# Weight conversion spread differently over the first batch: first weight from chunk 1 on, its scratch in another buffer, more of the second beside the first products, unread products in the mixing's wait

## Chip, cores and metric

The kernel runs on one core of one Trainium2 chip. The time is the device time of an execution in microseconds (us). The engines are named as in the profile: PE (TensorE, matmul; PEld its weight loads), DVE (VectorE), ACT (ScalarE), POOL (GpSimd) and SP (SyncE, which only issues DMAs here).

## The reference, cut to what matters

```python
# attention: B=4, H=8, S=768, D=48, a recurrence over time
for t in range(S):
    y[:, :, t] = q_t @ state
    state += beta_t * outer(kn_t, v_t - kn_t @ state)      # kn = normalized key
x = y, heads side by side                                  # (4, 768, 384)
# mixing and channel network
u = x + real(fft2(x))                                      # over sequence and channels
un = (u - mean) / sqrt(var + 1e-6)
out = u + relu(un @ w_ch1) @ w_ch2                         # 384 -> 1536 -> 384
```

The two weights lie in memory as 64-bit floats (the inputs are numpy's float64), [...]. So the kernel converts them itself, from pairs of 32-bit words.

## The kernel before

**Attention in chunks.** Each batch of 768 rows is cut into 6 chunks of 128 rows (`NL` = 6), so there are 24 chunks. Four chunks form a round, and each round needs the inversion of many small triangular matrices, which DVE does step by step (`invert16` with lines L519 and L522 for rounds 0 to 2, `invert` with L448 and L452 for rounds 3 to 5). An inversion begins with the transpose L477 (or L407) and ends with the transposes L525 and L527 (or L455, L456). For each chunk, `pre_a` turns the keys and forms their Gram matrices, `pre_q` turns the queries and makes the masked product `LQ` (L557), `pre_m16` or `pre_m` makes the matrix `MT` (PE products `one<-Z,GU`, `one<-MT,ND`, `one<-Z,ND`; DVE lines L647 and L651), `step` carries the state through the two halves of the chunk (DVE lines L722 or L700, and L741), and `outputs` forms the rows of `x`.

**Mixing and network.** When a batch has its rows, `folds` makes sums and differences of rows and columns on DVE (L797 to L815), `fourier` multiplies by tables (PE `pf`/`one<-evt`, `odt`, then `one<-dtab,F`), adds the result to `x` and takes mean and variance (L884 to L892). `mlp` normalizes (L911, tile `un`), turns on PE (`ptr`) and ACT (L922, tile `unT`), and makes the first products `ph`, evicted by ACT as `hT` (L932), and the second products `po`. The network is done in three groups of 256 rows per batch; a group has 12 first products of three matmuls each. In the trace each fp32 matmul counts as two instructions.

**Order.** All is written in the order in which it shall run: generators stop at `yield`, and `advance`, `drain` and lists of them weave chunks, inversions and network together. PE's, DVE's, ACT's and POOL's order is the written one (`manual_schedule`). For chunks 6 and 7 only PE's order is written, and a scheduler sets that of the others. SP's order of DMAs is the scheduler's as well.

**The conversion** is the generator `weights()`: 12 pieces of 128x384 numbers for `w1`, then 12 for `w2`. A piece is loaded (64-bit, 384 KB) into a ring and takes two half-steps. On ACT: L278 (low word), later L283 and L284 (exponent). On DVE: L279 (upper mantissa), then L295, L299 and L301, and L291, the product that writes the result. L291 comes one half-step pair after L301 of its piece for `w1` (two scratch tiles), two pairs after for `w2` (three). Scratch for `w1` are two pool buffers: tag `M`, of which there is one and which each inversion needs, and tag `unT`, of which there are two. For `w2` ring and scratch lie in tiles `E` and `O3` of batch 0's folds. `convert(n)` takes half-steps of `w1`: none in chunk 0 and 1, 5 in chunk 2, 6 in chunk 3, 4 in chunk 4, then 7 around the mixing and the rest among the first products:

```python
rest = [ms[6], k1, ms[7], k1, ms[7], ms[6], k2, ms[7], k2, ms[7], k3, k3]
for fc in range(KF):
    if converted < 2 * KF + 2:
        convert(2)
    else:
        advance(conv)
    advance(side)
```

`conv` then goes on in `period(6)`, beside the third inversion.

**Unread products.** `spin(n)` issues n products of 128x384 that nothing reads, three at the start and six before the first `pre_m16`. They have one PSUM buffer of the two of tag `post` and read a tile of zeros, `idle`.

Of the kernel before, what the change touches and what calls it, by code (L numbers as in the profile page):

```python
# [10 lines left out]
F32 = mybir.dt.float32  # L11
I32 = mybir.dt.int32
U32 = mybir.dt.uint32
AX = mybir.AxisListType
ALU = mybir.AluOpType
ACT = mybir.ActivationFunctionType
# [48 lines left out]
def kernel(  # L65
# [10 lines left out]
    nc = tc.nc  # L76
    B, H, S, D = q.shape
    DM = H * D
    DFF = moe_w_ch1.shape[1]
    NL = S // L  # L80
# [3 lines left out]
    KF = DFF // 128  # L84
# [11 lines left out]
    wk = ctx.enter_context(tc.tile_pool(name="wk", bufs=1))  # L96
# [9 lines left out]
    def ps_post(shape, name):  # L106
        return ps.tile(shape, F32, tag="post", bufs=2, name=name)
# [83 lines left out]
    w2 = const.tile([128, KF, DM], F32, name="w2")  # L191

    early = w2.rearrange("p c m -> p (c m)").rearrange("p (n h d) -> p n h d", h=8, d=64)
    idle = wk.tile([128, DM], F32, tag="un", bufs=2, name="idle")
# [15 lines left out]
    evt = const.tile([128, TH, 2 * NE], F32, name="evt")  # L210
    odt = const.tile([128, TH, 2 * NO], F32, name="odt")
    dtab = const.tile([ND + 1, 4, ND + 1], F32, name="dtab")
    w1 = const.tile([128, KD, DFF], F32, name="w1")
# [7 lines left out]
    half_n = const.tile([128, GT], F32, name="half_n")  # L221
    nc.gpsimd.memset(half_n, -0.5)

    def weights():

        if moe_w_ch1.dtype == F32:
            nc.sync.dma_start(out=w1, in_=moe_w_ch1.rearrange("(c p) f -> p c f", p=128))
            nc.sync.dma_start(out=w2, in_=moe_w_ch2.rearrange("(c p) m -> p c m", p=128))  # L230
            return
        w1v = moe_w_ch1.bitcast(I32).rearrange("(c p) (f two) -> p c f two", p=128, two=2)
        w2v = moe_w_ch2.bitcast(I32).rearrange("(c p) (m two) -> p c m two", p=128, two=2)
        n = DM
        sets = [
            [(w1v[:, :, i:i + 128], w1[:, :, i:i + 128]) for i in range(0, DFF, 128)],
            [(w2v[:, i:i + 1], w2[:, i:i + 1]) for i in range(KF)]]
        for last, pieces in enumerate(sets):
            if last:

                E, O3 = spare.pop()
                ring = E.rearrange("p e t m -> p (e t m)").bitcast(I32).rearrange(
                    "p (i m two) -> p i m two", m=n, two=2)
                tmp = O3.rearrange("p e t m -> p (e t m)").rearrange("p (i e m) -> p i e m", e=2,
                                                                    m=n)
                tmp = [tmp[:, i] for i in range(3)]
                deep = 3
            else:
                ring = wk.tile([128, 4, n, 2], I32, tag="big", bufs=2, name="w64")
                tmp = None  # L250
                deep = 4

            def stage(i):
                if i < len(pieces):
                    src = pieces[i][0]
                    nc.sync.dma_start(
                        out=ring[:, i % deep].rearrange("p (c f) two -> p c f two",
                                                        c=src.shape[1]), in_=src)

            for i in range(deep):  # L260
                stage(i)
            yield
            if tmp is None:
                tmp = [wk.tile([128, 2, n], F32, tag="M", name="wtmp0"),
                       wk.tile([128, 2, n], F32, tag="unT", bufs=2, name="wtmp1")]

            def of(i):
                t = tmp[i % len(tmp)]
                return ring[:, i % deep, :, 0], ring[:, i % deep, :, 1], t[:, 0], t[:, 1].bitcast(I32)


            lag = len(tmp) - 1
            for i in range(len(pieces) + lag):
                if i < len(pieces):
                    lo, hi, man, num = of(i)


                    nc.scalar.activation(man, lo.bitcast(U32), ACT.Copy, scale=2.0 ** -52, bias=1.0)  # L278
                    nc.vector.tensor_scalar(num, hi, 0xFFFFF, None, op0=ALU.bitwise_and)  # L279
                if 0 < i <= len(pieces):  # L280

                    num0 = of(i - 1)[3]
                    nc.scalar.activation(num0, num0, ACT.Relu, scale=-1.0, bias=edges[:, 0:1])  # L283
                    nc.scalar.activation(num0, num0, ACT.Relu, scale=-2.0 ** 23,  # L284
                                         bias=edges[:, 1:2])
                yield
                if i >= lag:
                    _, _, man0, num0 = of(i - lag)
                    dst = pieces[i - lag][1]
                    c = dst.shape[1]  # L290
                    nc.vector.tensor_tensor(dst, man0.rearrange("p (c f) -> p c f", c=c),  # L291
                                            num0.bitcast(F32).rearrange("p (c f) -> p c f", c=c),
                                            op=ALU.mult)
                if i < len(pieces):
                    nc.vector.scalar_tensor_tensor(man, num, 2.0 ** -20, man, op0=ALU.mult,  # L295
                                                   op1=ALU.add)

                    man = man.bitcast(I32)
                    nc.vector.scalar_tensor_tensor(man, hi, -2 ** 31, man, op0=ALU.bitwise_and,  # L299
                                                   op1=ALU.bitwise_or)  # L300
                    nc.vector.tensor_scalar(num, hi, 20, 0x7FF, op0=ALU.logical_shift_right,  # L301
                                            op1=ALU.bitwise_and)
                    stage(i + deep)
                yield

# [510 lines left out]
    folded, spare = {}, []  # L818
# [141 lines left out]
    def advance(gen, n=1):  # L960
        for _ in range(n):
            if next(gen, "end") == "end":
                return False
        return True

    def drain(gen):
        for _ in gen:
            pass
# [20 lines left out]
    def part(gen, n):  # L989

        for _ in range(n):
            if next(gen, "end") == "end":
                return
            yield
# [7 lines left out]
    def period(g, side):  # L1002
# [48 lines left out]
        for i in range(SLOTS):  # L1051
# [9 lines left out]
            if li == 1 and i == 1 and r > 1 and not last_round:  # L1061
                inv = invert(r + 1)
            if g == NL:
                advance(inv, 4)
                advance(conv, 3 if i < 4 else 4)
            elif inv:
                advance(inv, 8 if r + 1 < R16 else 6)
            if n + 2 >= NL and 0 < i < 5:
# [21 lines left out]
    with tc.manual_schedule(engines=engines):  # L1090
# [3 lines left out]
        inv0, inv1 = invert16(0), invert16(1)  # L1094
        qs = [pre_q(g, QT6[:, g], LQ6[:, g]) for g in range(NL)]
        ms = [pre_m16(g) for g in range(2 * RL)]
        unread = ps_post([128, 512], "unread")

        def spin(n):

            for _ in range(n):
                nc.tensor.matmul(unread[:, 0:DM], lhsT=idle[:, 0:128], rhs=idle, start=True,  # L1102
                                 stop=True, skip_group_check=True)

        spin(3)
# [13 lines left out]
        load_v(1, nc.gpsimd)  # L1119
        load_q(4)  # L1120
        load_q(5)
        conv = weights()
        advance(conv)

        for g in range(RL, 2 * RL - 1):
# [7 lines left out]
        drain(inv0)  # L1133
        advance(keys[-1])
        spin(6)

        advance(ms[0])
        drain(keys[-1])
# [10 lines left out]
        advance(ms[1])  # L1149
        drain(ms[0])  # L1150
        advance(inv1, 5)
        first = part(conv, 2 * KF + 2)
        converted = 0
        fold = fd = iter(())

        def convert(n):
            nonlocal converted
            advance(first, n)
            converted += n

        def fill(n):

# [6 lines left out]
        for g in range(NL - 1):  # L1169
# [22 lines left out]
            else:  # L1192
                advance(c0)
                fill(4)
                if g == 2:
                    drain(inv1)
                    advance(n2)
                if g > 1:
                    convert(1)
                advance(nm)  # L1200
                advance(late)
                advance(c0)
# [7 lines left out]
                advance(nm)  # L1210
                advance(c1)
                fill(3)
                if g > 1:
                    convert(2)
                drain(nm)
                advance(n2)
                advance(c1)
                fill(3)
                if g == 4:
                    advance(n2)  # L1220
                    drain(qs[g + 1])
                    convert(1)
                elif g > 1:
                    convert(1)
                    advance(n2)
                    convert(2 if g == 3 else 1)
                else:
                    advance(n2)
                if g != 4:
                    drain(qs[g + 1])  # L1230
                if g + 2 < NL:
                    advance(qs[g + 2])
# [13 lines left out]
        g = NL - 1  # L1246
# [16 lines left out]
        load_beta(2)  # L1263

        advance(ms[6])
        f = fourier(0)
        advance(f)
        drain(fold)
        convert(1)
        advance(f, 4)  # L1270
        convert(1)
        advance(f, 2)
        side, done = mlp(0), 0
        advance(side)
        advance(ms[6])
        advance(ms[7])
        advance(side)
        convert(3)
        advance(ms[7])
        convert(2)  # L1280

        k1, k2, k3 = keys[1:]
        rest = [ms[6], k1, ms[7], k1, ms[7], ms[6], k2, ms[7], k2, ms[7], k3, k3]
        for fc in range(KF):
            if converted < 2 * KF + 2:
                convert(2)
            else:
                advance(conv)
            advance(side)
            if fc % 3 == 1:  # L1290
                advance(f)
            drain(rest[fc]) if fc == 5 else advance(rest[fc])
        drain(f)
        nq = pre_q(NL)
        advance(nq)
        for m in ms[6:] + keys[1:]:
            drain(m)
        advance(side)
# [54 lines left out]
```

## Time and profile before

| | us |
|---|---|
| median of 3 runs | 760.12 (756.09 to 760.19) |
| profiled execution | 761.02 |
| its span, first to last instruction | 758.9 |
| PE busy | 696.9 (92%) |
| DVE busy | 378.6 (50%) |
| ACT busy | 263.7 (35%) |
| POOL busy | 69.7 (9%) |

The shares are means over stages with different limits, so a stage is read from its own stretch of time. Batch 0's steps run from about 45 to 121 us, its mixing from 121 to 138, its first group of first products from 142 to 176; batches 1 to 3 follow. A line of a group gives busy time, mean ns of one instruction, and idle time before it; a line of the timeline gives start, duration and, in brackets, the idle time before and what ended it.

### The profile page before, as it was taken

To read this page: it belongs to the slowest core of one execution; us is meant where nothing else is said; L and a number is where in the kernel's file an instruction comes from. 1 tells how busy PE (TensorE), PEld (TensorE's weight loads), DVE (VectorE), ACT (ScalarE), POOL (GpSimd) and SP (SyncE) were. 2 spreads that over 40 slices of the span, in tenths; PEclk is the share of its full clock that TensorE was granted. 3 is DMA by queue.
4 is the path that set the end of the run, shared out by engine and by line. 5 is a ranking of instruction groups with operands and counts; after the bars stand their busy time and mean duration, and the time that the engine had idled before them with its cause. 6 is when DMAs were issued, how large, how long until landed. Compare 5 with 4: busy or idle time off the path is not lost.

```text
span 758.9 us, 23039 instructions
## 1 busy us (share of the span) xinstructions
PE 696.9 (92%) x10170; PEld 538.0 (71%) x10170; DVE 378.6 (50%) x957; ACT 263.7 (35%) x644; POOL 69.7 (9%) x114
## 2 busy tenths in 40 slices
PE   6877879598989987999999999999999999999998
PEld 4677868476767655877857767868667678777684
DVE  5867776669932499433198327278512240600000
ACT  5544663568623321223422323223223221211120
POOL 7000000100000011001110210020100110100000
PEclk8698797799999999999999999999999999999999
DMA  9842352014312322002222211001220000000000
GB/s 152 215 74 41 88 135 83 18 54 124 87 29 55 60 44 44 12 11 47 52 45 48 44 34 39 1 13 42 43 44 12 13 12 0 22 1 21 11 10 22
DMA packets 111862, 36.09 MB, mean 48 GB/s; under 512 B 101873, under 2 KB 109842, under 8 KB 111762
## 3 DMA queue, kind: packets, MB, share of 16 engines
q1 hardware_dynamic: 109938, 33.86, 20.5%
q8 instruction: 80, 1.31, 0.7%
q0 software_dynamic: 640, 0.43, 0.4%
q10 hardware_dynamic: 1184, 0.33, 0.3%
q14 instruction: 20, 0.16, 0.1%
HBM read 29.88 MB, written 4.72 MB: 46 GB/s over the span
## 4 chain that ended last, share of the span: by engine, by line
PE 75%; DVE 16%; ACT 5%; issue 2%; DMA 1%; POOL 0%; DVEq 0%; ACTq 0%; POOLq 0%
PE po L110 23%; PE ph L110 21%; PE one L110 16%; PE pair L110 10%; PE one L113 2%; DVE M L452 1%; DVE tmp L448 1%; DVE w L291 1%; PE ptr L113 1%; PE unread L1102 1%; PE pf L110 1%; DMA C<-in_k_dram 1%; DVE M L522 1%; DVE Z L647 1%; DVE tmp L519 1%
## 5 line engine op out<-in xcount | busy, mean ns | idle before, releaser
L110 PE MATMUL ph<-unT,w 128*128 128x256 f32 x864 | 207.7, 392 | 2.8 <-ACT hT L932 2.0
L110 PE MATMUL po<-w,hT 128*128 128x384 f32 x576 | 205.1, 495 | 0.0
L110 PEld LDWEIGHTS ph<-unT,w 128*128 128x128 f32 x864 | 162.4, 194 | 27.6 <-ACT hT L932 2.4
L110 PEld LDWEIGHTS po<-w,hT 128*128 128x128 f32 x576 | 103.7, 190 | 56.7 <-issue 0.3
L932 ACT ACTIVATE hT<-ph 128x256 f32<-128x256 f32 x144 | 54.9, 382 | 145.0 <-PE ph L110 144.9
L943 DVE TENSOR_TENSOR x<-x,po 128x384 f32<-128x384 f32 x24 | 13.2, 550 | 107.0 <-PE po L110 107.0
L741 DVE TENSOR_TENSOR S<-S,pair 128x192 f32<-128x192 f32 x40 | 14.0, 349 | 73.9 <-PE pair L110 73.9
L110 PEld LDWEIGHTS one<-V,MT 64*64 64x64 f32 x768 | 30.5, 141 | 19.5 <-issue 9.2
L884 DVE TENSOR_TENSOR x<-x,one 128x193 f32<-128x193 f32 x24 | 8.5, 354 | 69.8 <-ACT Q L875 69.8
L110 PE MATMUL one<-V,MT 64*64 64x48 f32 x768 | 35.7, 227 | 3.6 <-DVE V L700 1.8
L452 DVE TENSOR_TENSOR M<-M,tmp 128x31 f32<-128x31 f32 (+15 forms) x93 | 34.7, 373 | 3.2
L448 DVE TENSOR_TENSOR tmp<-A,M 128x31 f32<-128x31 f32 (+15 forms) x93 | 34.2, 367 | 2.5
L110 PE MATMUL one<-MT,ND 64*64 64x64 f32 x768 | 30.4, 231 | 5.0 <-DVE x L885 2.6
L110 PEld LDWEIGHTS one<-MT,ND 64*64 64x64 f32 x768 | 27.8, 146 | 6.0 <-ACT Q L875 3.0
L700 DVE TENSOR_TENSOR V<-V,pair 128x192 f32<-128x192 f32 x33 | 11.5, 350 | 38.7 <-PE pair L110 35.4
L110 PEld LDWEIGHTS one<-dtab,F 97*128 97x128 f32 (+1 forms) x192 | 25.2, 191 | 5.2 <-ACT F L879 0.5
L110 PEld LDWEIGHTS pair<-U,K 64*64 64x64 f32 x704 | 16.6, 139 | 17.4 <-issue 14.9
L322 ACT ACTIVATE QT<-one 128x512 f32<-128x512 f32 x24 | 14.3, 594 | 38.9 <-PE one L113 38.7
L110 PE MATMUL one<-dtab,F 97*128 97x97 f32 (+1 forms) x192 | 25.9, 275 | 0.0
L110 PE MATMUL pair<-KT 48*32 48x64 f32 (+1 forms) x1152 | 21.1, 238 | 5.1 <-ACT KT L322 3.8
L110 PEld LDWEIGHTS pair<-S,KT 48*64 48x64 f32 x528 | 10.7, 133 | 20.1 <-issue 10.8
L710 ACT ACTIVATE U<-one 128x192 f32<-128x192 f32 x36 | 11.9, 330 | 37.7 <-PE one L110 37.7
(176 smaller groups left out, 1003.0 us busy)
## 6 DMA issues: line engine op xcount, KB each, us to landing
w<-in_moe_w_ch_dram SPq DMA_DIRECT2D x12, 384.0 KB, 5.6
E<-in_moe_w_ch_dram SPq DMA_DIRECT2D x12, 384.0 KB, 4.3
out_dram<-x SPq DMA_DIRECT2D x24, 192.0 KB, 1.9
K<-in_k_dram SPq DMA_DIRECT2D x92, 48.0 KB, 2.7
V<-in_v_dram SPq DMA_DIRECT2D x92, 48.0 KB, 2.2
C<-in_k_dram SPq DMA_DIRECT2D x18, 192.0 KB, 9.3
Q<-in_q_dram SPq DMA_DIRECT2D x18, 192.0 KB, 3.1
w<-in_q_dram SPq DMA_DIRECT2D x6, 192.0 KB, 7.5
```

Source lines behind the costliest of these rows:

```text
L110: nc.tensor.matmul(o, lhsT=lhsT, rhs=rhs, start=start, stop=stop, skip_group_check=True)
L113: nc.tensor.matmul(o, lhsT=src, rhs=ident[0:src.shape[0], 0:src.shape[0]], is_transpose=True, start=start, stop=True, skip_group_check=True)
L291: nc.vector.tensor_tensor(dst, man0.rearrange("p (c f) -> p c f", c=c), num0.bitcast(F32).rearrange("p (c f) -> p c f", c=c), op=ALU.mult)
L322: nc.scalar.activation(dst.rearrange("p h j t -> p (h j t)"), pt, ACT.Copy)
L448: nc.vector.tensor_tensor(t, A[:, j + 1:W, j:j + 1].broadcast_to([128, n, j + 1]), M[:, j:j + 1, 0:j + 1].broadcast_to([128, n, j + 1]), o ...
L452: nc.vector.tensor_tensor(M[:, j + 1:W, 0:j + 1], M[:, j + 1:W, 0:j + 1], t, op=ALU.add)
L700: nc.vector.tensor_tensor(R4, R4, pw[:, :, 0:2 * D].rearrange("p a (j e) -> p a j e", e=D), op=ALU.subtract)
L710: nc.scalar.activation(U.rearrange("p j e -> p (j e)"), pu[:, 0:4 * D], ACT.Copy)
L741: nc.vector.tensor_tensor(s1v, s0.rearrange("p h j e -> p h (j e)"), pk, op=ALU.add)
L884: nc.vector.tensor_tensor(near, near, pb[:, 0, 0:MH + 1], op=ALU.add)
L932: nc.scalar.activation(hT[:, fc, :], ph, ACT.Relu)
L943: nc.vector.tensor_tensor(x[:, T, :], x[:, T, :], po, op=ALU.add)
```

## The change

1. `weights()` becomes `weight(last)`, one generator for each weight. The scratch of `w1` is the first third of `w2`, where keys of chunks 5 to 7 had lain until they were turned; the tags `M` and `unT` are no longer used for it.
2. The conversion of `w1` begins in chunk 1: 5, 6, 6 and 4 half-steps in chunks 1 to 4, also set at other places within a chunk. One follows after the fold and the last four (`drain(conv)`) before the first products.
3. `w2`'s first loads are issued in the mixing, and its half-steps run beside all 12 first products, one or two for each. In `period(6)` there are 2 per slot (4 in the last) instead of 3 (4 in the last two), and 5 steps of the inversion per slot instead of 4.
4. `pre_m16` of chunks 6 and 7 moves forward, into the mixing and the first products' beginning; the turning of chunk 6's queries moves from behind the first products to among them.
5. `spin` takes a `post` buffer at each call. Two unread products are added in chunk 4, and twice six between the mixing's first sums and the turning of the first normalized rows; these read the table `evt` instead of the tile of zeros.

```diff
-    def weights():
+    def weight(last):
...
-            if tmp is None:
-                tmp = [wk.tile([128, 2, n], F32, tag="M", name="wtmp0"),
-                       wk.tile([128, 2, n], F32, tag="unT", bufs=2, name="wtmp1")]
+            tmp = w2[:, 0:4].rearrange("p (i e) m -> p i e m", e=2)
+            tmp = [tmp[:, i] for i in range(2)]
+            deep = 4
...
             if g == NL:
-                advance(inv, 4)
-                advance(conv, 3 if i < 4 else 4)
+                advance(inv, 5)
+                advance(conv, 2 if i < 5 else 4)
...
         def spin(n):
 
+            unread = ps_post([128, 512], "unread")
+            src = idle if idle is not None else evt[:, 0, 0:DM]
             for _ in range(n):
-                nc.tensor.matmul(unread[:, 0:DM], lhsT=idle[:, 0:128], rhs=idle, start=True,
+                nc.tensor.matmul(unread[:, 0:DM], lhsT=src[:, 0:128], rhs=src, start=True,
                                  stop=True, skip_group_check=True)
...
-                if g > 1:
-                    convert(1)
+                convert(1)
                 advance(nm)
                 advance(late)
                 advance(c0)
...
                 fill(3)
-                if g > 1:
-                    convert(2)
+                convert(1)
                 drain(nm)
...
                 if g == 4:
+                    spin(2)
                     advance(n2)
                     drain(qs[g + 1])
-                    convert(1)
-                elif g > 1:
-                    convert(1)
+                    convert(2)
+                else:
+                    convert(1 if g == 1 else 2)
                     advance(n2)
-                    convert(2 if g == 3 else 1)
-                else:
-                    advance(n2)
-                if g != 4:
+                    convert(2)
                     drain(qs[g + 1])
...
         advance(ms[6])
+        advance(ms[7])
         f = fourier(0)
         advance(f)
         drain(fold)
         convert(1)
         advance(f, 4)
-        convert(1)
+        w2s = weight(1)
+        advance(w2s)
         advance(f, 2)
         side, done = mlp(0), 0
+        advance(ms[7])
+        advance(ms[6])
         advance(side)
-        advance(ms[6])
+        spin(6)
         advance(ms[7])
+        spin(6)
         advance(side)
-        convert(3)
-        advance(ms[7])
-        convert(2)
-
+        drain(conv)
+        conv = w2s
+
+        nq = pre_q(NL)
         k1, k2, k3 = keys[1:]
-        rest = [ms[6], k1, ms[7], k1, ms[7], ms[6], k2, ms[7], k2, ms[7], k3, k3]
+        rest = [k1, ms[7], k1, ms[7], k2, ms[7], k2, k3, nq, k3]
         for fc in range(KF):
-            if converted < 2 * KF + 2:
-                convert(2)
-            else:
-                advance(conv)
             advance(side)
+            advance(conv, 2 if fc % 3 == 2 else 1)
             if fc % 3 == 1:
                 advance(f)
-            drain(rest[fc]) if fc == 5 else advance(rest[fc])
+            if fc < len(rest):
+                advance(rest[fc])
         drain(f)
-        nq = pre_q(NL)
-        advance(nq)
```

## The prediction

> **What bounds the kernel now.** I read the page's slices first, then the stretches of 10 us, then the timeline from 40 to 225 us.
>
> ```profile
> span 758.9 us, 23039 instructions
> ...
> PE   6877879598989987999999999999999999999998
> ...
> DVE  5867776669932499433198327278512240600000
> ...
> PEclk8698797799999999999999999999999999999999
> ```
>
> A slice is 19 us. From the twelfth on (210 us) PE is 90% busy or more: batches 1 to 3, which the change doesn't touch. The earlier slices have holes and a reduced clock. So the change is worth what it moves the moment, near 212 us, from which every engine has its old order.
>
> ```profile
> 120.00:130.00 10.00, 10.00 (x74) 9.60 (x72) 7.71 (x19) 1.12 (x4) 0.00 (x0) 0.81 0.19 57
> 130.00:140.00 10.00, 4.10 (x26) 3.31 (x24) 5.66 (x17) 4.49 (x12) 1.09 (x3) 0.70 0.30 100
> 140.00:150.00 10.00, 8.02 (x61) 6.92 (x61) 6.68 (x17) 7.18 (x14) 0.46 (x1) 0.79 0.11 22
> 150.00:160.00 10.00, 7.38 (x84) 5.68 (x83) 5.54 (x14) 6.51 (x17) 0.52 (x1) 0.83 0.13 42
> 190.00:200.00 10.00, 10.00 (x87) 8.30 (x81) 10.00 (x32) 8.40 (x19) 1.49 (x1) 1.00 0.46 133
> ```
>
> Columns: PE, PEld, DVE, ACT, POOL busy, PE clock, DMA. The hole is at 130 to 160: the mixing, then first products slowed by the first weight's conversion. From 180 to 210 DVE is full: second weight and third inversion.
>
> ```profile
> 81.96 0.69 DVE L647 TENSOR_TENSOR Z<-MT,one 128x512 f32<-128x512 f32 x1 [2.83 <-PE pair L110]
> 138.56 1.54 PE L113 MATMUL ptr<-pack,un 128*128 128x128 f32 x6 [5.90 <-DVE un L911]
> 142.49 0.56 DVE L291 TENSOR_TENSOR w<-wtmp 128x384 f32<-128x384 f32 x1 [1.06 <-ACT wtmp L284]
> 149.22 1.56 PE L110 MATMUL ph<-unT,w 128*128 128x256 f32 x6 [1.98 <-ACT hT L932]
> 178.56 1.94 DVE L477 STREAM_TRANSPOSE A<-G 128x1024 f32<-128x1024 f32 x1
> 210.35 1.87 DVE L527 STREAM_TRANSPOSE A<-M 128x1024 f32<-128x1024 f32 x1
> 212.47 1.11 PE L110 MATMUL pair<-QT,KT 48*64 48x64 f32 x32 [3.34 <-DVE S L741]
> ```
>
> Start, duration, in brackets the idle before. These are my marks: the transposes `ptr` at 138.56, the third inversion from 178.56 to 212.22, PE at 212.47. Prices:
>
> ```profile
> L279 DVE TENSOR_SCALAR wtmp<-w 128x384 int32<-128x384 int32 x12 | 4.2, 353 | 0.0
> L291 DVE TENSOR_TENSOR w<-wtmp 128x384 f32<-128x384 f32 x12 | 6.7, 555 | 5.7 <-ACT wtmp L284 5.7
> L295 DVE SCALAR_TENSOR_TENSOR wtmp<-wtmp 128x384 f32<-128x384 int32 x12 | 6.6, 552 | 0.0
> L299 DVE SCALAR_TENSOR_TENSOR wtmp<-w,wtmp 128x384 int32<-128x384 int32 x12 | 6.7, 558 | 0.4
> L301 DVE TENSOR_SCALAR wtmp<-w 128x384 int32<-128x384 int32 x12 | 4.2, 353 | 0.0
> ```
>
> One piece is 2.37 us of DVE durations; started one behind the other (87.31, 87.78, 88.37, 88.85, 89.11) they take 2.1. On ACT it is L278, L283, L284: 0.55+0.61+0.61, 1.65 us in a row.
>
> **What the Trainium skill says.** "Trainium Architecture — The Big Picture", section "Inside one NeuronCore": each engine has its own instruction stream, and they meet only through semaphores. So an `hT` eviction behind L284 in ACT's stream waits for DVE's L301 with it; the trace agrees (1.98 us at 149.22). "TensorE: Matmul & The Clock Gate", section "What's actually happening": the clock is halved by default, freed after about 3.4 us of activity and halved after about as long idle. The trace agrees: `ptr` x6 takes 1.54 us after 5.90 idle and 0.82 at 181.09; 32 instructions of `Z,GU` behind it 1.97 against 1.05 at 88.42. "VectorE: DVE Perf Modes", section "The DRAIN you can't avoid", says the next operation starts only when the pipe is empty; here L295 starts 0.47 us after L291 of 0.55, so I take starts.
>
> **The change, part by part,** with the order of instructions of both kernels. No conversion instruction is added or removed; 14 unread products are.
>
> *Conversion in the steps of batch 0.* Half-steps by chunk go from 0, 5, 6, 4 (chunks 1 to 4) to 5, 6, 6, 4: three pieces, 7.1 us of DVE, go ahead of the fold. Chunk 1: L295, L299, L301 fall into the 3.0 us before L647 (65.65), free. But 2.4 us go before `LQ` (68.15), where 1.2 is idle, and 2.0 instead of 0.3 behind L527, before the `MT` and `S` that PE waits for, where 1.1 is idle: +1.9. Chunk 2: the 2.83 idle at 81.96 stays unused, as only L279 stands there; between `S` and `LQ` stand two pieces instead of one, and the second's L291 waits, as at 142.49, 1.06 for L283 and L284: 2.1+1.1 less 0.7 idle, +2.5. Chunk 3: the same pair, against one piece before L647 and one after: +2.1. Chunk 4: a piece leaves L647 (-1.5) and comes before `U` (+1.7); two unread products (4 instructions of 0.32, as `po` of the same shape at full clock, 12 in 3.87) lie in PE's wait for L647 but for some 0.5, which a PE wait of 1.07 for no shown cause (114.40) takes: 0. After that only PE's order counts. Fold end: +6.5. Lower bound +1, if DVE's idle time (6.5 us in 80 to 110) takes it; upper +8.
>
> *Scratch in the place of keys 5 to 7.* Those were last read near 26 us; the waits named for PE's query transposes are the old ones. Nothing. POOL's clearing of `M` for the third inversion loses its 11.4 us wait, but is needed only by 178. SP now issues the loads of pieces before key and value loads of chunks two ahead; a step lasts some 12 us and a load lands in 5.6, four pieces ahead: nothing, at most +1.
>
> *The mixing's wait.* `Q` no longer stands behind L278 to L284 (131.11 to 132.80), L279 is gone and the V product sits in POOL's 1.15 wait: `un` 0.9 earlier. But PE now has, behind `dtab` (ending 132.66), `Z,GU` 1.05, six unread products 3.87 (12 instructions), `MT,ND` 1.05, six more 3.87: 9.84, with handovers 10.1, against 5.9. So `ptr` waits for PE itself and is 4.2 later, offset +10.7; it runs at full clock (-0.7), and `Z,GU` (1.97) behind it is gone. Lower bound 0, if the mixing's sums come late enough to cover them; upper +8, if part of the 24 runs at half clock.
>
> *The loop of first products.* Before, 40.0 us from `ptr` to L477. Here ACT is the limit. In its new order between `unT` and L477: 12 `hT` 4.4, 9 L278 and 9 pairs L283/L284 15.3, 3 `KT` 1.5, 3 evictions of G and GU 6.1, 4 `Q` 1.3, mirrors 1.75, `MT` and `QT` 1.0: 31.3. Before them come 1.4 (`ptr`, `unT`), and 2.0 are lost once, when piece 11 waits for its own L301; the last items (`GU`, one `hT`, one `Q`) come after L477, -1.4. So 33.3, -6.7. PE (26 us of work) and DVE (27.9 of durations, 24 in starts) lie beside it. L477: +10.7-6.7 = +4.0. Lower bound 31 (no waits), upper 42 (ACT's former busy share: 31.3 over 0.75).
>
> *The third inversion.* L477 to the end of L527 was 33.7 us, DVE full, 39.5 of durations; now 36.8 (three steps fewer of the second weight, one mixing tile more). Times 33.7/39.5: 31.4, and 1 for L291s behind ACT: 32.4, -1.3. L527 ends at +2.7, near 215.
>
> *What is late next.* Five inversion steps per slot instead of four put `V` (L700) behind L527; it stood at 202.26, ten us ahead. From L527 PE must now do `V,MT` and `S,QT` 1.1, `po` x8 2.6, `U,K` 0.3, with L700 and L741 0.7 and handovers 0.3: 5.0 to `QT,KT`, where it was 0.25: +4.75. But PE no longer idles 3.34 us there, so `QT,KT`, `Z,GU` and `po` x8 run at 0.6+1.05+2.6, not 1.1+1.95+3.2: -2.0. Sum: +2.7+4.75-2.0 = +5.5. The query products of chunk 6 only change their place.
>
> The profiled execution is 761.0 (span 758.9 and 2.1 around it), the median of the runs 760.1. +5.5 gives 766.5 and 765.6; I take 766.
>
> **Rivals.** *The loop stays as long* (slower). ACT's queue holds `hT`, `Q`, G evictions and conversions in one order, each L283 waits for DVE, which waits for mixing sums from PE, which waits for `hT`. For: ACT was busy only 29.9 of 40 us in 140 to 180. Against: over a third of that idle time lay beside the one-deep pieces of the first weight, to 152. Price: 41.7 instead of 33.3, +8.4: 774.5. It decides once `ptr` to L477 passes 40 us.
>
> *The pieces cost only idle time* (faster). Each conversion runs in time that DVE and ACT would have idled, in the steps and in the loop: the fold shifts by +1 instead of +6.5, the 2.0 lost on piece 11 and the 1 of L291s behind ACT go. 8.5 less: 757.5, under the time before. For: DVE idles 6.6 us in 60 to 80 and 6.5 in 80 to 110, ACT more. Against: much of that lies ahead of PE's results, not where the pieces stand. It ends on this side once the fold ends before 127.5, since 5.5 must go.
>
> *The unread products do not do what they are for*: `ptr` finds the clock full without them. Then they only hold it: in my sum already but for the 0.7.
>
> **How the numbers follow.** Forecast 0.46 (761 to 771); loop stays 0.26 (771 to 780); idle time only 0.28 (748 to 761). A third of the first lies over 767.7 (0.16), all of the second, and 0.12 of the last under 752.5 (the unread products covered too, 4.2): faster by over 1% 0.12, within 1% (about what a measurement tells from no change) 0.46, slower by over 1% 0.42. Range 752 to 776, with about a tenth on either side.
>
> **What would show it.** Right: L815 of the fold ends near 132.4 (was 125.9); `ptr` near 149 straight behind unread products, 0.8 us long; L477 near 182.5; L527 ends near 215, with L700 right behind; `QT,KT` near 220. Wrong: a fold before 129, idle time ahead of `ptr`, a `ptr` to L477 of over 40 us, or any difference that arises after 225 us.

## The result and the profile after

The changed kernel took 765.5 us, the median of four runs (764.77 to 767.2), against 758.11 for the kernel before in four (755.73 to 760.19): a ratio of 1.0102, with an interval of 1.0058 to 1.0145. So it is slower, by 1%. Its profiled execution took 767.2 us with a span of 765.3; that of before was 761.02 with 758.9. The difference between the two, 6.2 us, is what the steps below must add up to.

The page of the changed kernel, the same rows as before:

```profile
span 765.3 us, 23096 instructions
...
PE   7876788996999987899999999999999999999998
...
DVE  5868667479842299625188426369511230700000
...
PEclk8699678998899999999999999999999999999999
```

From 210 us on (twelfth slice) PE is busy for nine tenths or more, but for slices 15 to 17 (8, 7 and 8) and the last. Before, slices 12, 15 and 16 stood at 8, 8 and 7, so the prediction's "90% busy or more" was too broad; its use of it holds, as the difference lies ahead of that moment. Stretches of 10 us of the changed kernel, in the prediction's columns:

```profile
120.00:130.00 10.00, 6.86 (x222) 6.26 (x223) 7.77 (x20) 5.48 (x13) 0.00 (x0) 0.71 0.17 33
130.00:140.00 10.00, 10.00 (x67) 9.51 (x65) 6.42 (x16) 2.37 (x9) 0.00 (x0) 0.95 0.35 116
140.00:150.00 10.00, 9.72 (x92) 6.53 (x92) 6.06 (x17) 1.93 (x5) 1.42 (x3) 1.00 0.02 4
150.00:160.00 10.00, 7.51 (x68) 6.11 (x67) 4.27 (x11) 6.25 (x15) 0.00 (x0) 1.00 0.11 22
190.00:200.00 10.00, 10.00 (x92) 7.95 (x90) 8.22 (x30) 5.95 (x14) 0.00 (x0) 0.71 0.27 86
```

In 130 to 140 PE is full because the mixing's matmuls now lie there, nine us later than before. From 142 to 151 it is filled with unread products: a full PE row here is not work. In 150 to 160 it is as open as before (7.51 against 7.38). From 190 to 200 DVE is no longer full, and the clock is at 0.71. The timeline's lines at the marks (start, duration, idle before and what ended it):

```profile
83.66 0.69 DVE L645 TENSOR_TENSOR Z<-MT,one 128x512 f32<-128x512 f32 x1 [4.01 <-PE pair L110]
134.50 0.36 DVE L813 TENSOR_TENSOR O<-O 128x190 f32<-128x190 f32 x1
145.53 0.87 DVE L909 TENSOR_SCALAR un<-x,mv,rstd 128x384 f32<-128x384 f32 x2 [0.92 <-POOL rstd L894]
147.23 4.14 PE L1101 MATMUL unread<-evt 128*128 128x384 f32 x12
151.20 0.82 PE L113 MATMUL ptr<-pack,un 128*128 128x128 f32 x6
181.91 1.99 DVE L475 STREAM_TRANSPOSE A<-G 128x1024 f32<-128x1024 f32 x1 [0.33 <-ACT G L385]
213.59 1.92 DVE L525 STREAM_TRANSPOSE A<-M 128x1024 f32<-128x1024 f32 x1
215.35 0.34 DVE L698 TENSOR_TENSOR V<-V,pair 128x192 f32<-128x192 f32 x1
220.54 0.69 PE L110 MATMUL pair<-QT,KT 48*64 48x64 f32 x32
226.31 0.69 DVE L645 TENSOR_TENSOR Z<-MT,one 128x512 f32<-128x512 f32 x1 [0.56 <-PE one L110]
```

And of the kernel before, the end of the fold and that last L645 (there L647):

```profile
125.56 0.36 DVE L815 TENSOR_TENSOR O<-O 128x190 f32<-128x190 f32 x1
219.84 0.69 DVE L647 TENSOR_TENSOR Z<-MT,one 128x512 f32<-128x512 f32 x1 [0.63 <-PE one L110]
```

`ptr` follows the second six unread products without a gap, at full clock, while its input `un` had been ready since 146.4. V (L698) stands right behind L525. L645 of a chunk of batch 1 comes 6.5 us later than L647 did, and +6.4 is left at the end of the span. The marks, as offsets against the profile before (lengths of a step are differences of two offsets):

| mark | predicted | measured | the step's own share, predicted | measured |
|---|---|---|---|---|
| fold ends | +6.5 | +8.9 | +6.5 | +8.9 |
| `ptr` | +10.7 | +12.6 | +4.2 | +3.7 |
| L475 (third inversion begins) | +4.0 | +3.4 | -6.7 | -9.3 |
| L525 ends | +2.7 | +3.3 | -1.3 | -0.1 |
| `QT,KT` | +7.5 | +8.1 | +4.8 | +4.8 |
| behind it, to the end | +5.5 | +6.5 | -2.0 | -1.6 |

### The profile page after: what moved, and what is told of

Same layout as the page of the kernel before. It is cut to its first block, busy times and chain, and to the rows that moved or that the text cites. A ratio compares the mean times of both kernels' runs of the same rounds, so it can differ in the third digit from the quotient of the medians.

```text
span 765.3 us, 23096 instructions
## 1 busy us (share of the span) xinstructions
PE 705.3 (92%) x10198; PEld 542.2 (71%) x10198; DVE 378.1 (49%) x957; ACT 264.3 (35%) x644; POOL 71.2 (9%) x114
## 4 chain that ended last, share of the span: by engine, by line
PE 76%; DVE 15%; ACT 6%; issue 2%; DMA 1%; SPq 0%; ACTq 0%; DVEq 0%
PE po L110 24%; PE ph L110 21%; PE one L110 15%; PE pair L110 10%; PE one L113 2%; PE unread L1101 2%; DVE M L450 1%; DVE tmp L446 1%; PE ptr L113 1%; DVE w L289 1%; DMA C<-in_k_dram 1%; DVE M L520 1%; ACT G L385 1%; DVE tmp L517 1%; PE pf L110 1%
## 5 line engine op out<-in xcount | busy, mean ns | idle before, releaser
L110 PEld LDWEIGHTS one<-V,MT 64*64 64x64 f32 x768 | 32.4, 147 | 20.0 <-issue 8.3
L110 PE MATMUL one<-V,MT 64*64 64x48 f32 x768 | 37.7, 234 | 4.2 <-DVE V L698 2.7
L882 DVE TENSOR_TENSOR x<-x,one 128x193 f32<-128x193 f32 x24 | 8.5, 353 | 63.2 <-ACT Q L873 63.2
L698 DVE TENSOR_TENSOR V<-V,pair 128x192 f32<-128x192 f32 x33 | 11.5, 349 | 38.8 <-PE pair L110 30.6
L110 PEld LDWEIGHTS pair<-U,K 64*64 64x64 f32 x704 | 15.8, 139 | 16.6 <-issue 12.7
L893 POOL TENSOR_SCALAR rstd<-mv 128x2 f32<-128x2 f32 x12 | 3.9, 325 | 249.4 <-DVE mv L890 249.4
L110 PEld LDWEIGHTS pair<-S,KT 48*64 48x64 f32 x528 | 10.7, 133 | 21.7 <-issue 10.6
```

What stands on the lines that cost most here:

```text
L110: nc.tensor.matmul(o, lhsT=lhsT, rhs=rhs, start=start, stop=stop, skip_group_check=True)
L698: nc.vector.tensor_tensor(R4, R4, pw[:, :, 0:2 * D].rearrange("p a (j e) -> p a j e", e=D), op=ALU.subtract)
L882: nc.vector.tensor_tensor(near, near, pb[:, 0, 0:MH + 1], op=ALU.add)
```

## The experiments

Ratios are to the kernel before on the same chip, with 95% intervals. The median of before in the three groups of experiments was 756.23, 757.87 and 758.07 us. The first four start from the changed kernel.

**1. No unread products in the mixing.**

```diff
         advance(side)
-        spin(6)
         advance(ms[7])
-        spin(6)
         advance(side)
```

> The changed kernel without its two times six unread products in the mixing; the instructions of the other engines keep their order. Theory (they hold PE): un ends at 146.4 as before, ptr starts within 0.3 us of it instead of at 151.2, at half clock (1.5 us for six); the loop of first products is bound by ACT, so L475 follows at 178.5 to 180 (181.9 in the changed kernel), and the time falls by 2 to 4 us, to about 762.5. Rival (they pay for themselves): the first products run at half clock for 10 us, the loop from ptr to L475 grows by the 4 to 5 us that ptr gains, and the time stays at 765.5.

760.83 us, ratio 1.0052 (1.0031 to 1.0072), under the changed kernel's 1.0102. The timeline of this kernel:

```profile
145.59 0.94 PE L113 MATMUL ptr<-pack,un 128*128 128x128 f32 x6 [1.28 <-DVE un L909]
176.33 2.00 DVE L475 STREAM_TRANSPOSE A<-G 128x1024 f32<-128x1024 f32 x1 [0.33 <-ACT G L385]
```

From `ptr` to L475 it is 30.7 us, as with the products (181.91 less 151.20). So the gain at `ptr` is kept whole, 5.2 us against the end of the fold in the two profiles. By the two ratios the twelve products cost about 3.8 us, and they gave nothing back. One detail of the theory failed: `ptr` was not at half clock, it took 0.94 us, near the 0.82 with the products. The clock fell only behind it (0.72 up to 150 us, 0.90 from there to 155), and the loop was no longer for it.

**2. Half-steps in the chunks as before.**

```diff
-                convert(1)
+                if g > 1:
+                    convert(1)
...
-                convert(1)
+                if g > 1:
+                    convert(2)
...
-        drain(conv)
-        conv = w2s
+        convert(6)
...
-            advance(conv, 2 if fc % 3 == 2 else 1)
+            if fc < 2:
+                convert(2)
+            else:
+                if fc == 2:
+                    drain(conv)
+                    conv = w2s
+                advance(conv, 2 if fc % 3 == 2 else 1)
```

> The changed kernel with the half-steps of the first weight placed as in the kernel before (0, 5, 6, 4 in chunks 1 to 4, six ahead of the first products, the last four among the first two of these, the second weight from the third on). V (L698) comes between the two last transposes of the third inversion instead of behind them, which by itself is worth up to 2 us. Theory (pieces ahead of the fold cost chunks 1 to 3 their time): the third L813 ends near 126.5 instead of 134.9, ptr comes 7 to 8 earlier, and the loop from ptr to L475 grows from 30.7 to 35 to 37 for the two pieces that it gets: together with V a time of about 761. Rival (a piece costs the same wherever it stands): the loop grows by the whole 8 us, to 39, and the time stays within 764 to 766.

759.04 us, 1.0043 (1.0022 to 1.0064). The fold ended at 119.4, 15.5 us earlier than in the changed kernel, where the theory had 8, and 6.5 earlier than in the profile of before with the same half-steps. The loop from `ptr` to L475 took 37.6 us (135.22 to 172.81), 6.9 more and a little over the 35 to 37 of the theory. Pieces in the chunks thus cost more than in the loop; but why the fold beat that of the kernel before was open, and experiments 7 and 10 were made for it.

**3. V one transpose earlier.**

```diff
-                advance(inv, 5)
                 advance(conv, 2 if i < 5 else 4)
+                advance(inv, 5)
```

> The changed kernel with two lines exchanged in the first period of batch 1: in each slot the half-steps of the second weight are written ahead of the steps of the inversion, with the same counts. The scheduler then puts V (L698) between the two last transposes of the third inversion, one transpose of 1.92 us earlier. Theory (V behind L525 is what PE waits for at the end of the third inversion): QT,KT comes about 2 us earlier, from 220.5 to 218.5, and the time falls by 1.5 to 2, to 763.7. Rival (something else holds PE there, or the queue of L739 and the products behind it takes the 2 us back): 765.5.

766.62 us, 1.0127 (1.009 to 1.0164): no gain. V came at 213.04, ahead of L525, and PE's `V,MT` ran at 214.01 without a wait. `QT,KT` started 3.6 us behind L525's end (215.23 to 218.80), instead of 5.0. A gain of 1.5 us at that place is thus there in the profile, but not in the times, whose interval is wider than that. The time is as the rival had it.

**4. Two unread products in chunk 3.**

```diff
                 convert(1)
+                if g == 3:
+                    spin(1)
                 advance(nm)
+                if g == 3:
+                    spin(1)
                 advance(late)
```

> The changed kernel with two more unread products in chunk 3, one ahead of MT,ND (which waits 1.18 us for ACT at 88.25) and one ahead of S,QT (1.17 us for LQ at 90.57), 0.65 us each at full clock, so that they fit into these waits. Theory (chunk 2 to 3 lost 2 us more than worked out because PE idled in 86 to 91 and got the halved clock in 91 to 100): the clock stays full to beyond 96, L645 at 100.77 comes about 2 us earlier, the fold too, and the time falls by 1 to 2, to 764. Rival (the halved stretch only begins later and lasts as long): the fold ends at 134.5 to 135.5, the time stays at 765.5.

761.41 us, 1.0058 (1.0023 to 1.0093). The stretch from 90 to 100 us, of the changed kernel and then of this one:

```profile
90.00:100.00 10.00, 8.87 (x214) 8.39 (x216) 5.05 (x12) 6.31 (x14) 0.00 (x0) 0.50 0.34 92
```

```profile
90.00:100.00 10.00, 7.79 (x308) 7.23 (x308) 7.19 (x18) 6.47 (x15) 0.00 (x0) 1.00 0.44 107
```

The clock goes from 0.50 to 1.00, and PE ends 308 instructions instead of 214. The two waits, in the changed kernel and then in this one:

```profile
88.25 1.15 PE L110 MATMUL one<-MT,ND 64*64 64x64 f32 x32 [1.18 <-ACT MT L647]
90.57 1.11 PE L110 MATMUL pair<-S,QT 48*64 48x48 f32 x32 [1.17 <-DVE LQ L555]
```

```profile
87.59 1.15 PE L110 MATMUL one<-MT,ND 64*64 64x64 f32 x32 [0.33 <-ACT MT L647]
89.91 0.68 PE L110 MATMUL pair<-S,QT 48*64 48x48 f32 x32 [0.32 <-DVE LQ L555]
```

Both come 0.66 us earlier here, but so does L645 ahead of the edit (83.00 instead of 83.66): the products themselves cost nothing. L645 then comes at 97.17 instead of 100.77, of which 2.9 arise behind the products, and the fold ends 3.9 us earlier. The theory is right, with a size above its 1 to 2. It is not chance of one execution: from L649 of chunk 2 to that of chunk 3 it takes 14.16 us in both kernels with these products (experiments 4 and 6), and 16.6 to 17.3 in all six that have the early pieces without them. Here two products lie in waits of PE; the twelve of the mixing were longer than the wait that they lay in.

**5. Experiments 1 and 2 together.**

> Both of the first two edits at once: half-steps of the first weight in the chunks as in the kernel before, and no unread products in the mixing. Theory (the two gains lie one behind the other, the pieces in the chunks, the products between un and ptr): ptr starts at once behind un, 4.8 us earlier than in the second experiment, and its 759.0 becomes 754.5 to 755.5, at or just under the kernel before. Rival (with PE cold and six pieces' half-steps right behind, the loop now takes the gain): 758 to 760.

753.72 us, 0.9951 (0.9928 to 0.9973): faster than both kernels. `ptr` starts at 129.01 where experiment 2 had 135.22. Of the change it keeps the scratch, the second weight's half-steps beside the first products, the counts in `period(6)`, the moved `pre_m16` and query products, and the two unread products of chunk 4; which of these make it faster than the kernel before was not tried one by one. From `ptr` to L475 it takes 38.6 us.

**6. Experiments 1 and 4 together.**

> The changed kernel with the two unread products in chunk 3 and without the twelve in the mixing. Theory (both gains are separate): about 4 us from each, 757 to 758, with fold end near 131 and ptr near 142. Rival (without the twelve the halved clock of the mixing reaches into the loop and the loop takes the gain): 760.5 to 761.5.

757.96 us, 1.0003 (0.9979 to 1.0026), fold end at 131.2, `ptr` at 142.4: the two gains add up. From experiment 5 to this one 4.2 us are lost: the price of the pieces in the chunks without the twelve products, and with the two in chunk 3.

**7. The scratch alone**, in the kernel before.

```diff
-                tmp = [wk.tile([128, 2, n], F32, tag="M", name="wtmp0"),
-                       wk.tile([128, 2, n], F32, tag="unT", bufs=2, name="wtmp1")]
+                t4 = w2[:, 0:4].rearrange("p (i e) m -> p i e m", e=2)
+                tmp = [t4[:, i] for i in range(2)]
```

> The kernel before with one part of the change alone: the scratch of the first weight in the first third of the second weight, nothing else moved. Theory: the inversions no longer share tag M with it, but nothing that PE waits for changes: within 0.3% of the kernel before. Rival (the second experiment's chunk 1 was 2.6 us ahead of the kernel before with the same half-steps): L647 of chunk 2 comes at 63 instead of 65.65 and the time falls by 2 us or more.

757.19 us, 1.0007 (0.9977 to 1.0037): no effect that the interval shows. PE, DVE and ACT have the order of the kernel before; of POOL's work the clearing of `M` for the third inversion moves from 149.5 to 71.9 us. L647 did come at 63.46, as the rival said, but the time did not fall with it. Yet this one's profiled execution took 754.7 us, and its fold ended at 118.82, 7.1 us ahead of the profile before. Stretches of the kernel before, then of this one:

```profile
70.00:80.00 10.00, 7.15 (x195) 6.71 (x188) 7.97 (x13) 4.74 (x10) 0.20 (x1) 0.63 0.07 14
80.00:90.00 10.00, 9.46 (x278) 8.91 (x274) 6.60 (x15) 5.46 (x12) 0.00 (x0) 0.69 0.43 109
110.00:120.00 10.00, 8.00 (x257) 7.33 (x254) 5.67 (x15) 5.15 (x12) 0.00 (x0) 0.51 0.30 69
```

```profile
70.00:80.00 10.00, 7.80 (x256) 7.43 (x256) 7.92 (x16) 5.93 (x13) 1.19 (x2) 0.83 0.24 59
80.00:90.00 10.00, 7.70 (x299) 6.99 (x293) 8.39 (x21) 8.45 (x18) 0.00 (x0) 1.00 0.51 122
110.00:120.00 10.00, 9.56 (x129) 9.20 (x130) 9.16 (x22) 1.86 (x6) 0.00 (x0) 0.75 0.15 41
```

The clock is the last but two of the columns. With one and the same order it was 0.63 and 0.69 from 70 to 90 us in one execution, 0.83 and 1.00 in the other. The runs of both kernels spread widely, 752.7 to 763.6 and 753.3 to 761.6, and the two profiled executions lie at different places of that spread.

**8. No unread products in chunk 4** (the changed kernel without `spin(2)`).

> The changed kernel without the two unread products in chunk 4. Theory (they lie in a wait of PE and cost nothing, but keep the clock full from 114 to 122): without them chunk 4 runs at the halved clock, the third L813 ends 1 to 3 us later than 134.9, the time goes to 766.5 to 768. Rival (they only hold PE, 1.3 us): the fold ends a little earlier, the time is 764 to 765.5.

766.47 us, 1.0123 (1.0067 to 1.0178), not to be told from the changed kernel, so the rival's gain isn't there either. From L645 of chunk 4 to the end of the fold it took 17.2 us (114.44 to 131.68), against 18.4 with them (116.47 to 134.86). The theory falls: they save nothing there. A wait of PE is thus not enough for such products to pay.

**9. Experiment 5 with the second weight's half-steps as before in the first period.**

```diff
-                advance(conv, 2 if i < 5 else 4)
+                advance(conv, 3 if i < 4 else 4)
```

> The fifth experiment's kernel with 3 half-steps of the second weight in the first four slots of the first period of batch 1, as in the kernel before, instead of 2; the scheduler then puts V (L698) ahead of both last transposes of the third inversion, with two pairs of L517 and L520 between. Theory (PE waits there for V): from the end of L525 to QT,KT it takes 0.3 us as in the kernel before, instead of 2.7, and the time falls by 1 to 2.5, to 751.5 to 752.5. Rival (the place of V was paid back elsewhere, as in the third experiment, whose time did not fall): 753.5 to 754.

754.87 us, 0.9941 (0.9917 to 0.9966): within the interval of experiment 5. V came 2.9 us ahead of L525, and still `QT,KT` started 2.3 us behind L525's end (206.58 to 208.88), because PE was busy up to it but for one wait of 0.31. The theory falls; the rival, that the time does not fall, is right.

**10. Early pieces alone**: experiment 7's kernel with the half-steps 5, 6, 6, 4.

```diff
-                if g > 1:
-                    convert(1)
+                convert(1)
...
-                if g > 1:
-                    convert(2)
+                convert(1)
...
-                    convert(1)
-                elif g > 1:
-                    convert(1)
-                    advance(n2)
-                    convert(2 if g == 3 else 1)
-                else:
-                    advance(n2)
+                    convert(2)
+                else:
+                    convert(1 if g == 1 else 2)
+                    advance(n2)
+                    convert(2)
```

> The kernel of the seventh experiment with one more part of the change: half-steps of the first weight as in the changed kernel (5, 6, 6, 4 in chunks 1 to 4) and so all of it done ahead of the first products, the second weight one half-step for each of these; no unread products. DVE's order up to the fold is that of the changed kernel. Theory (three pieces cost the chunks about 12 us at the clock of the seventh experiment, the loop gives back some 8): fold end at 130 to 135, the loop from ptr to L477 at 31 to 33, the time 761 to 763. Rival (the chunks only lose what the halved clock takes): fold end within 124 to 126 and the time 753 to 755.

759.93 us, 1.0028 (1.0014 to 1.0043), a little under what the theory gave. Its timeline:

```profile
130.77 0.36 DVE L815 TENSOR_TENSOR O<-O 128x190 f32<-128x190 f32 x1
143.50 1.54 PE L113 MATMUL ptr<-pack,un 128*128 128x128 f32 x6 [5.91 <-DVE un L911]
176.81 1.93 DVE L477 STREAM_TRANSPOSE A<-G 128x1024 f32<-128x1024 f32 x1 [0.16 <-ACT G L387]
```

The fold ends at 131.13, 12.3 us behind experiment 7. The loop takes 33.3 us, a little over the 31 to 33 of the theory, against 40.1 there (130.67 to 170.78): 6.8 come back.

**11. One piece of chunk 2 behind LQ.**

```diff
                     advance(n2)
-                    convert(2)
+                    convert(2 if g != 2 else 0)
                     drain(qs[g + 1])
+                    convert(2 if g == 2 else 0)
```

> The changed kernel with one piece of the pair in chunk 2 moved behind L555 (LQ), which PE's S,QT waits for; nothing else changes place. Theory (the pair ahead of LQ makes PE idle, and with that the clock falls): LQ comes 2 us earlier in chunk 2, the halved stretch of 90 to 100 shortens or goes, the fold ends 2 to 4 us earlier than 134.9 and the time is 762 to 764. Rival (DVE is full there, what stands behind LQ delays U and MT as much): the fold within 134 to 135.5, the time 765 to 766.

766.39 us, 1.011 (1.0077 to 1.0143), no gain. LQ came 4.6 us earlier in chunk 2 (85.22 instead of 89.83), the next L645 only 1.9 (98.88), and the fold 1.9 (132.95), most of it already there ahead of the edit: L645 at 65.15 and 82.28, 1.2 and 1.4 earlier. The halved stretch became shorter (the clock is 0.66 in 90 to 100 instead of 0.50) and did not go; between the two L649 it saved 0.5 us. The piece delays what stands behind LQ instead.

## Why the prediction was right, and where it was not

The direction and the places were right. That 766 met 765.5 so closely was luck in part. The forecast added 5.5 us to a median of 760.1; the kernel before took 758.1 in the runs that the change was measured against, so the medians differ by 7.4 us and the profiled executions by 6.2. The single steps were off by up to 2.6 us in the profile, and their errors cancelled.

**Steps of batch 0: +6.5 predicted, +8.9 measured, and some 13 against other executions with the old half-steps.** This is the mis-sized term. From L645 (L647) of chunk 2 to the end of the fold it took

| half-steps | kernel | us |
|---|---|---|
| 0, 5, 6, 4 | before | 60.3 |
| 0, 5, 6, 4 | experiments 2, 5, 7, 9 | 56.4, 53.1, 55.4, 55.6 |
| 5, 6, 6, 4 | changed | 68.6 |
| 5, 6, 6, 4 | experiments 1, 3, 8, 10, 11 | 68.4, 68.3, 67.9, 67.7, 67.8 |
| 5, 6, 6, 4, two products in chunk 3 | experiments 4, 6 | 65.1, 65.1 |

The three early pieces and their order cost some 13 us here (12.3 between experiments 7 and 10), of which 3 went with the halved clock of chunk 3. By chunk, from L651 to L651 (L649 in the changed kernel), the two profiles differ by 2.5, 0.7, 5.4 and -0.1 us in chunks 1 to 4, where 1.9, 2.5, 2.1 and 0 were worked out; 0.5 more lay ahead of chunk 1.

In chunk 2 the profile before hid a cost. PE ran at half clock from 72 to 86 us there and DVE idled for it, and the chunk took 14.9 us. In experiments 2, 5, 7 and 9 the same half-steps took 10.7 to 11.9, and with the early pieces it is 15.4 to 15.7 in every kernel that has them (in the changed one with a halved stretch of its own, from about 76 to 83). The prediction took starts and waits from that one profile, and so took for granted cover that other executions don't have. In chunk 3 it had no term for what a longer wait of PE does to the clock behind it: experiment 4 takes 3.0 of the 5.4 away. The rival that the pieces cost only idle time is ruled out by the fold (134.9, not under 127.5).

**Scratch: 0.** Experiment 7 shows no effect, within 0.3% (2 to 3 us) either way.

**The mixing's wait: +4.2 predicted, +3.7 measured.** Right with its reason: `ptr` waits for PE itself. `un` came 1.4 earlier against the fold, not 0.9. The third rival held as well: without the products `ptr` found the clock nearly full (0.94 us in experiment 1), and the reduced clock behind it didn't lengthen the loop. In experiments 2 and 5, with `ptr` at 0.82 and 1.41 us, the loops took 37.6 and 38.6; so in these two profiles a slower `ptr` goes with about 1 us more of loop, and starts 6.2 us earlier.

**The loop: 33.3 predicted, 30.7 measured.** ACT sets most of its length, as said: in the profile's chain of waits from 152.6 to 181.9 it has 16.1 us, DVE 8.7 and PE 2.7. But the sum of its durations, 31.3, was too large. Of the loop, changed kernel:

```profile
151.20:181.90 30.70, 26.82 (x287) 22.72 (x285) 22.68 (x58) 26.27 (x63) 1.41 (x4) 1.00 0.37 103
```

ACT is busy for 26.27 us in it. An ACT instruction starts while the one before it is still counted: L276 at 77.38 takes 0.54, and L281 behind it starts at 77.82. For DVE the prediction took starts, for ACT durations; the same rule was due to both. The 2.0 lost once on piece 11 are there (1.96 ahead of L281 at 156.15). The rival of a loop that stays at 40 us is ruled out. Experiment 10 shows how the gain divides: 6.8 from the pieces, the other 2.6 from the rest of the change. These 2.6 are not kept: from `ptr` to the end of the span it takes 613.2 us in experiment 10 and 613.4 in experiment 1, which has the rest of the change too. In part they are work moved behind the mark, as the next step shows.

**The third inversion: 32.4 predicted, 33.6 measured.** DVE was not full as assumed, busy for 31.1 of 33.6 us. First three lines of the kernel before, then the changed kernel:

```profile
174.96 0.35 DVE L884 TENSOR_TENSOR x<-x,one 128x193 f32<-128x193 f32 x1
177.56 0.86 DVE L911 TENSOR_SCALAR un<-x,mv,rstd 128x384 f32<-128x384 f32 x2
181.09 0.82 PE L113 MATMUL ptr<-pack,un 128*128 128x128 f32 x6
```

```profile
183.82 0.32 DVE L882 TENSOR_TENSOR x<-x,one 128x193 f32<-128x193 f32 x1
188.68 0.86 DVE L909 TENSOR_SCALAR un<-x,mv,rstd 128x384 f32<-128x384 f32 x2
189.30 1.09 PE L113 MATMUL ptr<-pack,un 128*128 128x128 f32 x4 [5.82 <-DVE un L909]
191.77 4.85 PE L110 MATMUL ph<-unT,w 128*128 128x256 f32 x12
197.09 0.36 DVE L737 COPY S<-pair 128x192 f32<-128x192 f32 x1 [1.78 <-PE pair L110]
```

The last tile of the mixing that the second group's `un` needs (from L884, now L882) stood ahead of L477 and now stands behind L475. So the second `ptr`, which ran at 181.09 without a wait, waits 5.82 us for `un`. Behind it PE is at half clock (12 `ph` in 4.85, then 12 in 2.86), and DVE waits 1.78 for it. The step that failed is the scaling of the old length by durations alone: the prediction counted "one mixing tile more" as DVE's time, and not that `ptr` waits for this tile.

**V behind L525: +4.8 and -2.0 predicted, +4.8 and -1.6 measured.** The size was right, the cause only in part, so the size was met by luck. The prediction gave it to five inversion steps per slot; but with two lines only exchanged, at the same counts, V moves (experiment 3), so the place is the scheduler's choice. And V is little of it:

```profile
215.75 0.49 PE L110 MATMUL one<-V,MT 64*64 64x48 f32 x10 [0.92 <-DVE V L698]
216.82 2.85 PE L110 MATMUL po<-w,hT 128*128 128x384 f32 x8
```

PE waits 0.92 us for V. The rest is `po` and other products that PE had not got to yet; its 5.82 idle and the half clock behind it are time enough for that, though no run took them away. With V early, `QT,KT` is still 2.3 to 3.6 us behind L525 (experiments 3, 5, 9).

Put together from ratios: early pieces with the scratch make 0.3% (experiment 10), the twelve products 0.5% (experiment 1). The 0.2% that is left of the 1.0% is less than the intervals, so nothing is shown for it.

## What to carry to other kernels

Work moved from a loop that an engine bounds into "idle" time of a chain costs what it delays there. Price it against several executions, as one profile can owe its idle time to a clock that the next does not have.

Unread products were added or taken out at three places here. They paid in chunk 3, where they fitted into two waits and the clock had been halved right behind. In chunk 4 they saved nothing, and in the mixing, where they were longer than the wait, they held back the start of a loop that did not need the clock.

A step that gets shorter between two marks may only have passed work behind its second mark, so look also at the end of the span. For ACT or DVE with many short instructions add up starts, or the busy time of a stretch, not durations.

## What the runs showed of the hardware

With the same order of PE, DVE and ACT, PE's clock was halved for about 14 us (72 to 86) in one execution, and for about 3.5 (from 70.7) in the execution of experiment 7; at the fold they are 7 us apart. The scratch need not be the reason: of 104 runs of the kernel before itself, from 752.2 to 763.6 us, the 68 with a mean granted clock of 0.96 or more have a median of 755.8 us, the other 36 of 759.8. What decides it between executions stays open.

Two unread products of 0.9 us of busy time each, which shortened two waits from 1.2 to 0.3 us, took away a halved stretch of 10 us.
